# Batch 0 of an attention and feed-forward kernel in program order, with w_out converted by column halves

## The chip, the cores and the metric

The kernel runs on 1 core of one Trainium2 chip. The metric is the device time of one execution in microseconds. TensorE is called PE, VectorE DVE, ScalarE ACT, GpSimd POOL and SyncE SP, as in the profile.

## The reference

```
S = 448; scores = q @ k.T / sqrt(64) - log(S)          # 8 batches, 12 heads, head size 64
attn = 1 / (1 + exp(-scores))
x = (attn @ v)  as [8*448, 768]                        # heads side by side
h = x @ w_in                                           # w_in 768 x 2048
out = (h - tanh(h)) @ w_out                            # w_out 2048 x 768
```

q, k, v are 32-bit floats. w_in and w_out arrive as 64-bit floats; the kernel reads them as pairs of 32-bit words.

## The kernel before

**Stages.** For each batch there is the attention (six pairs of heads, the four 112-row chunks of the keys per pair), a first product h = x @ w_in with the function g = h - tanh(h) (`mix`, L691: six passes on ACT and six on DVE for a pair of 128-column blocks, 448 tokens each), and a second product g @ w_out (`moe2`, L723: three tiles of 128 tokens, then the last 64 tokens as `por`). From batch 1 on, each 32-bit operand is split into two 16-bit parts with a power-of-two scale, and a product takes three 16-bit matmuls (batch 1 still has its product with v in 32 bits, AV32). Batch 0 has its attention and its first product in 32-bit matmuls, because the weights aren't there yet: they are loaded and converted during batch 0.

**Conversion of the weights** (`convert`, L190). A piece is loaded by SP (`conv_load`), ACT takes the absolute value of its high words (`conv_sign`, L143), DVE puts the bits together in three passes (`conv_bits`, L148, L149, L152), and its squares are taken for the scales. w_in has 24 pieces of 128 x 512; their squares are made alternately on POOL and ACT and summed by columns on PE (`cn`, L181). w_out has 32 pieces of 128 x 384, whose squares are summed by rows on ACT (L161). Each call of `next` on this generator does one step: it loads piece t and carries earlier pieces one stage on. Once a scale is known, `split` (L202) makes the two 16-bit parts of a piece: the first on ACT or DVE, the rest on DVE.

**Order.** Batch 0's attention (`attention32`) and first product (`moe1` with split=False) are written as generators, woven with the conversions by estimated costs (`weave`), and the order of the instructions on each engine is left to a planner. Everything from `first` on stands under `manual_schedule`, where PE, ACT, DVE and POOL get their instructions in the order of the program; SP, which starts the loads and stores, is always planned. The attention of batch b + 1 is a generator of blocks (`stream`, L410): five steps prepare the first two pairs of heads (loads, norms, scales, the parts of K and Q), then each block does the scores of two key chunks of a pair, their Sigmoid, the product with v of the two before, and part of the preparation of the next pair. `first` does three blocks, the scale of w_out (`w_out_scales`, L249) and the first splits. `second` (L871) then runs `moe2` step by step: after step n all events with a position up to n are done. Events are blocks (BLOCKS0 for batch 0), splits of w_in (SPLIT: position of the first, distance) and the scales of the next batch's x (`batch_scales`, L583). The splits of w_out stand in `moe2` itself, one row block per step (`ahead`).

**Buffers that matter.** PSUM has two pairs of banks for scores and ph (tag sc), two banks for po, products of batch 0's attention and norms (mm), one for transposes (tr) and one for the products with v (av). SBUF tag t has eight large buffers for Sigmoids and the passes of `mix`.

In batch 0's first product (L652) the transpose of the column sums of w_in (`w_in_scales`, L228) comes after the first pair of blocks in the program, and its second half with the scale of g (`g_scales`) in the second pair.

## Time and profile before

| | us |
|---|---|
| median of 3 runs | 1292.35 (1292.14 to 1292.64) |
| profiled execution | 1291.75 |
| its span | 1289.9 |
| first ph of batch 0 starts | 78.98 |
| first po of batch 0 starts | 196.89 |
| first ph of batch 1 starts | 303.29 |

The span runs from the first to the last instruction. L12 is line 12 of the kernel; kT, qT, sc, acc, ph, po and por are PSUM tiles, named by what writes them. In rows of a timeline stand the start, the length, the engine, the line, the operation with output and inputs, the count, and in brackets the idle time before with what ended it. In rows of a group the two numbers after the bar are the busy time in total and the mean of one in ns, then the idle time before them.

### The profile page before, as it was taken

What the parts mean: (1) busy time and instruction counts of PE and PEld (TensorE: products, weight loads), DVE (VectorE), ACT (ScalarE), POOL (GpSimd) and SP (SyncE); (2) the same over time, 40 slices, a digit from 0 to 9 for tenths busy, and PEclk for the clock granted to TensorE, in tenths of its full rate; (3) what the DMA queues carried; (4) which work ended last, traced back from release to release, by engine and by line L of the source; (5) the groups of instructions that cost most, each with busy time, mean ns of one, the idle gap of its engine ahead of it and who ended that gap; (6) DMA issues with size and microseconds to landing.
All of it is one profiled execution on the core that took longest, in us unless ns stands there. A gap on an engine that the chain in (4) does not pass through costs nothing.

```text
span 1289.9 us, 20436 instructions
## 1 busy us (share of the span) xinstructions
PE 1246.1 (97%) x7997; PEld 686.3 (53%) x7997; DVE 949.6 (74%) x1479; ACT 944.6 (73%) x1358; POOL 50.9 (4%) x50
## 2 busy tenths in 40 slices
PE   9899849989999999999999999999999999999998
PEld 3234425545555655555555655556555655555555
DVE  4889978785976879667976769667985779735940
ACT  6768868866888768886888868886888868763830
POOL 1210000100000000100001000000000000000000
PEclk9899959999999999999999999999999999999999
DMA  9863421211012200221012200221002210100001
GB/s 255 249 184 118 149 58 44 64 42 40 1 49 64 56 7 6 66 64 41 1 33 72 62 9 1 62 65 48 1 23 67 52 34 1 28 13 19 1 13 32
DMA packets 113888, 70.53 MB, mean 55 GB/s; under 512 B 91776, under 2 KB 103552, under 8 KB 113792
## 3 DMA queue, kind: packets, MB, share of 16 engines
q1 hardware_dynamic: 113792, 69.23, 20.0%
q8 instruction: 63, 1.03, 0.3%
q14 instruction: 33, 0.27, 0.1%
HBM read 58.20 MB, written 11.01 MB: 54 GB/s over the span
## 4 chain that ended last, share of the span: by engine, by line
PE 84%; DVE 7%; ACT 4%; issue 3%; DMA 1%; SPq 1%; ACTq 0%; DVEq 0%
PE ph L661 30%; PE po L752 29%; PE sc L345 8%; PE acc L369 7%; PE por L770 5%; PE acc L379 1%; PE kT L282 1%; PE qT L282 1%; DVE stb L149 1%; ACT a L354 1%; DVE wo L209 1%; DVE sta L149 1%; DVE wo L152 1%; PE sc L554 1%; DMA rawo<-moe_w_out 1%
## 5 line engine op out<-in xcount | busy, mean ns | idle before, releaser
L752 PE MATMUL po<-wo,g 128*128 128x384 f16 x2304 | 389.8, 326 | 1.8 <-ACT o L761 1.0
L661 PE MATMUL ph<-xhl,wi 128*128 128x448 f16 x2016 | 382.6, 352 | 0.0
L752 PEld LDWEIGHTS <-g 128*128 128x128 f16 x2304 | 219.6, 98 | 172.5 <-issue 32.0
L661 PEld LDWEIGHTS <-wi 128*128 128x128 f16 x2016 | 196.7, 98 | 185.0 <-issue 2.1
L354 ACT ACTIVATE a<-sc,nls,rn 112x896 f32<-112x896 f32 x168 | 179.7, 1095 | 72.4 <-PE sc L345 72.4
L361 DVE SCALAR_TENSOR_TENSOR ahl<-a,ahl 112x896 f16<-112x896 f32 x144 | 155.9, 1123 | 61.2 <-ACT ahl L360 61.2
L697 ACT ACTIVATE u<-ph,ih 128x896 f32<-128x896 f32 x64 | 64.4, 1006 | 96.1 <-PE ph L661 96.1
L360 ACT ACTIVATE ahl<-a 112x896 f16<-112x896 f32 x144 | 128.1, 939 | 0.0
L345 PE MATMUL sc<-Q,K 64*112 64x448 f16 x1008 | 116.9, 365 | 0.0
L701 DVE SCALAR_TENSOR_TENSOR m<-ph,ihk,u 128x896 f32<-128x896 f32 x64 | 73.4, 1146 | 58.0 <-ACT th L699 57.7
L369 PE MATMUL acc<-ahl,vhl 112*64 112x448 f16 x864 | 96.5, 357 | 0.1
L635 ACT ACTIVATE g<-m,Sg 128x896 f16<-128x896 f32 x64 | 66.7, 1042 | 38.6 <-DVE m L715 31.5
L323 DVE SCALAR_TENSOR_TENSOR Q<-qT,sn,Q 128x448 f16<-128x448 f32 x42 | 28.6, 682 | 75.8 <-ACT Q L320 75.8
L652 PE MATMUL ph<-x,wi 128*128 128x448 f32 x192 | 75.3, 551 | 6.7 <-DVE th L702 6.7
L715 DVE COPY_PREDICATED m<-u,th 128x896 f32<-128x896 uint32 x64 | 77.3, 1208 | 5.8
L636 DVE SCALAR_TENSOR_TENSOR g<-m,Sg,g 128x896 f16<-128x896 f32 x64 | 73.3, 1145 | 7.8 <-ACT g L635 7.8
L345 PEld LDWEIGHTS <-K 64*112 64x112 f16 x1008 | 60.4, 129 | 34.0 <-issue 4.5
L712 DVE SCALAR_TENSOR_TENSOR m<-q,m 128x896 f32<-128x896 f32 x64 | 69.9, 1092 | 6.8 <-DVE m L708 0.5
L702 DVE SCALAR_TENSOR_TENSOR th<-ph,ih,th 128x896 f32<-128x896 f32 x64 | 73.1, 1143 | 0.0
L708 DVE SCALAR_TENSOR_TENSOR m<-q,m 128x896 f32<-128x896 f32 x64 | 69.4, 1084 | 0.0
L369 PEld LDWEIGHTS <-vhl 112*64 112x64 f16 x864 | 43.3, 109 | 47.9 <-issue 26.0
L714 ACT ACTIVATE u<-u,b 128x896 f32<-128x896 f32 x64 | 66.6, 1041 | 1.8
(129 smaller groups left out, 1359.4 us busy)
## 6 DMA issues: line engine op xcount, KB each, us to landing
raw<-moe_w_in SPq DMA_DIRECT2D x24, 512.0 KB, 5.6
rawo<-moe_w_out SPq DMA_DIRECT2D x32, 384.0 KB, 3.5
kn<-k SPq DMA_DIRECT2D x96, 112.0 KB, 2.9
qn<-q SPq DMA_DIRECT2D x96, 112.0 KB, 2.9
vn<-v SPq DMA_DIRECT2D x48, 224.0 KB, 2.7
out<-o SPq DMA_DIRECT2D x8, 336.0 KB, 3.2
out<-o SPq DMA_DIRECT2D x8, 288.0 KB, 3.1
out<-o SPq DMA_DIRECT2D x8, 240.0 KB, 2.6
```

Of the source, the lines that this page charges most:

```text
L345: nc.tensor.matmul(ps[:CK, h, :S], K[r, w, cs], Q[r, x, :], start=(n == 0), stop=(n == len(prods) - 1))
L354: nc.scalar.activation(a, ps[:CK, :, :S], AF.Sigmoid, bias=self.nls[:CK], scale=scale)
L360: nc.scalar.activation(A[:, 0], a, AF.Copy, scale=A_SCALE)
L361: nc.vector.scalar_tensor_tensor(A[:, 1], a, A_SCALE, A[:, 0], op0=ALU.mult, op1=ALU.subtract)
L369: nc.tensor.matmul(acc[h * D : (h + 1) * D, : self.S], v[:, w, h, c, :], A[:, x, h], start=(c == 0 and n == 0), stop=(c == 3 and n == 2),)
L636: nc.vector.scalar_tensor_tensor(g[:, 1], m, Sg, g[:, 0], op0=ALU.mult, op1=ALU.subtract)
L652: nc.tensor.matmul(ph[:, e, :S], self.where("in", c)[:, f * P : (f + 1) * P], xhl[c], start=(c == 0), stop=(c == self.NC - 1),)
L661: nc.tensor.matmul(ph[:, e, :S], self.wi[:, c * self.NB + k, part, e * P : (e + 1) * P], xhl[c][:, x, :], start=(i == 0), stop=(i == 3 * s ...
L701: V.scalar_tensor_tensor(m, ps, ihk, u, op0=ALU.mult, op1=ALU.mult)
L702: V.scalar_tensor_tensor(th, ps, ih, th, op0=ALU.mult, op1=ALU.subtract)
L715: V.copy_predicated(m, u.bitcast(U32), th)
L752: nc.tensor.matmul(po[e][:, :H], gs[f // 2][:, x, f % 2, tk * P : (tk + 1) * P], self.wo[:, 2 * f + e, w], start=(f == 0 and n == 0), stop ...
```

## The change

All of batch 0 comes under `manual_schedule`: its attention, its first product (now `moe1_32`, a function of its own) and the passage are written out in the order in which each engine gets them, with the steps of the conversion at fixed places, and `weave` is gone. An ACT instruction at the very start loads the table for Sigmoid. K of batch 0 is copied from PSUM by DVE and Q by ACT (both by ACT before), and the transposes of Q use a bank of tag mm. Of the squares of w_in, a quarter are made on POOL. w_out lies in SBUF by column halves (row e * 16 + f where it was 2 * f + e; `where` follows), and its pieces are converted in that order: the first half within attention and first product, the second half within the second product, into buffers of tag t. The squares of w_out are gone: PE sums the absolute values by columns instead (`wl`, the high 16 bits of the converted piece times ones), and `w_out_scale` makes a scale for each half. The second product of batch 0 runs by column halves, one bank and three tiles each; its outputs are stored by halves, by ACT alone. In batches 1 to 7 only the factors of the outputs change: one per half. All splits of w_in have their first part on ACT. The five preparing steps of `stream` stand at pairs 0 and 3 to 6 of the first product; `first` does four blocks, and twelve follow in BLOCKS0.

```diff
-    LATE = 0.86
-    NMY = 3000
-    PACE = 1.1
-    INIT = 5
-    SPLIT = 13, 0.6
+    INIT = (0, 3, 4, 5, 6)
+    SPLIT = 13, 0.8
+    CONV = 0.9
...
-    BLOCKS0 = (3, 7, 11, 16, 19, 22, 25, 28, 32, 36, 44, 48, 52)
-    WI = 1.25
+    BLOCKS0 = (2, 4, 7, 10, 13, 16, 19, 23, 27, 36, 43, 50)
...
         for c in range(self.NC):
             for i in range(4):
                 yield ("in", c, i, n)
-        for f in range(self.NF):
-            for i in range(2):
+        for i in range(2):
+            for f in range(self.NF):
                 yield ("out", f, i, self.HALF)
...
             p["raw"] = self.stage.tile([P, n], U64, name="raw", tag="raw", bufs=5)
         else:
             pool, tag, bufs = (self.op, "o", 2) if p["k"] % 5 % 3 == 1 else (self.att, "vhl", 3)
+            if i:
+                pool, tag, bufs = self.tp, "t", self.TP
             p["raw"] = pool.tile([P, n], U64, name="rawo", tag=tag, bufs=bufs)
...
         if not p["staged"]:
-            junk = self.sm.tile([P, p["piece"][3]], BF16, name="sqo", tag="sq", bufs=4)
-            nc.scalar.activation(junk, p["F"], AF.Square, accum_out=self.won[:, k : k + 1])
             return
-        pool, tag, bufs = (self.stage, "ssq", 2) if k % 3 == 2 else (self.sm, "sq", 4)
-        p["sq"] = pool.tile([P, p["piece"][3]], BF16, name="sq", tag=tag, bufs=bufs)
-        if k % 2:
+        p["sq"] = self.sm.tile([P, p["piece"][3]], BF16, name="sq", tag="sq", bufs=4)
+        if k % 4 == 1:
             nc.gpsimd.tensor_tensor(p["sq"], p["F"], p["F"], op=ALU.mult)
         else:
             nc.scalar.activation(p["sq"], p["F"], AF.Square)
     def conv_end(self, p):
+        kind, r, i, n = p["piece"]
         if not p["staged"]:
+            if r == 0:
+                self.wl = self.ps.tile([P, 512], F32, name="wl", tag="mm", bufs=2)
+            high = p["a"].bitcast(BF16).rearrange("p (n t) -> p n t", t=2)[:, :, 1]
+            self.nc.tensor.matmul(self.wl[:, :n], self.onesb, high, start=(r == 0), stop=(r == self.NF - 1))
             return
-        kind, r, i, n = p["piece"]
...
     def convert(self, part):
-        stages = [self.conv_load, None, self.conv_sign, self.conv_bits, self.conv_norm, None, None, self.conv_end]
         ps = []
         for k, (q, staged) in enumerate(part):
             ps.append({"piece": q, "k": k, "staged": staged})
+        end = [self.conv_norm, None, self.conv_end] if ps[0]["staged"] else [self.conv_end]
+        wait = [None] * (1 if ps[0]["piece"][2] else 2)
+        stages = [self.conv_load] + wait + [self.conv_sign, self.conv_bits] + end
...
     def split_w_in(self):
         for n in range(self.NC * self.NB):
-            self.split(self.wi, n, self.Swi, n % 4 > 0)
+            self.split(self.wi, n, self.Swi, True)
             yield 1
...
-    def w_out_scales(self):
+    def w_out_scale(self, e):
+        V = self.nc.vector
+        m = self.sm.tile([P, 1], F32, name="mo")
+        V.tensor_reduce(m, self.wl[:, : self.HALF], axis=AX.X, op=ALU.max)
         total = self.sm.tile([P, 1], F32, name="wtot2")
-        self.nc.vector.tensor_reduce(total, self.won, axis=AX.X, op=ALU.add)
-        pw = self.ps.tile([P, 512], F32, name="pw", tag="tr", bufs=1)
-        self.nc.tensor.matmul(pw[:, :1], self.onesf, total, start=True, stop=True)
-        self.Swo, self.iSwo = self.scale_of(pw[:, :1], "swo")
-    def split_w_out(self):
-        for f in range(self.NF):
-            for e in range(2):
-                self.split(self.wo, 2 * f + e, self.Swo, e == 0 or f % 2 == 1)
+        V.scalar_tensor_tensor(total, m, 1.05, m, op0=ALU.mult, op1=ALU.mult)
+        S, inv = self.scale_of(total, f"swo{e}")
+        self.Swo.append(S)
+        V.tensor_copy(self.iSwo[:, e : e + 1], inv)
+        h = slice(e * D, (e + 1) * D)
+        V.tensor_copy(self.iSwo[h, 2:3], inv[h])
+    def split_w_out(self, e):
+        for f in range(0, self.NF, 2):
+            for n in (f, f + 1):
+                self.split(self.wo, e * self.NF + n, self.Swo[e], n % 4 > 0)
             yield 1
...
-                t = self.transpose(loaded[j][n], name + "T")
+                t = self.transpose(loaded[j][n], name + "T", *((), ("mm", 2))[n])
                 o = self.qk.tile([P, S], F32, name=name + "S", tag=name)
-                nc.scalar.activation(o, t, AF.Copy)
+                if n:
+                    nc.scalar.activation(o, t, AF.Copy)
+                else:
+                    nc.vector.tensor_copy(o, t)
...
-        yield 0
+        self.warm(14)
         qk = {0: prep(0)}
-        self.warm(14)
-        yield 900
+        self.warm(4)
...
-                yield 1520
+                next(weights, None)
                 if len(todo) > 2:
                     av()
-                    yield 760
                 if c == 1 and j + 1 < NP:
                     qk[j + 1] = prep(j + 1)
                     if j + 2 < NP:
                         loaded[j + 2] = load(j + 2)
-                    yield 900
+                if c == 3 and 0 < j < NP - 1:
+                    next(weights, None)
+                if c == 3 and j == NP - 1:
+                    next(rest)
         while todo:
+            next(weights, None)
+            next(rest)
             av()
-            yield 760
...
+    def moe1_32(self, xs, rest):
...
+        for k in range(self.NF // 2):
+            ph = self.ps.tile([P, 2, 512], F32, name="ph", tag="sc", bufs=2)
+            for e in range(2):
+                f = 2 * k + e
+                for c in range(self.NC):
+                    nc.tensor.matmul(
+                        ph[:, e, :S],
+                        self.where("in", c)[:, f * P : (f + 1) * P],
+                        xs[c],
+                        start=(c == 0),
+                        stop=(c == self.NC - 1),
+                    )
+                if e == 0 and k == 1:
+                    next(w, None)
                     self.Sg, self.iSg = self.g_scales(m)
...
+                if e == 0 and k in self.INIT:
+                    next(self.blocks)
+                for _ in range(2 if e and 0 < k < 4 else 1):
+                    next(rest, None)
+            g = self.gp.tile([P, 2, 2, S], F16, name="g", tag="g")
+            self.gs.append(g)
+            self.tail = self.mix(ph[:, :, :S], g, self.ih0, self.ihk0)
+            if k == self.NF // 2 - 1:
+                return
+            for _ in self.tail:
+                pass
+            if k == 0:
+                w = self.w_in_scales()
+                next(w)
+                m = self.token_norms(self.ps.tile([P, 512], F32, name="nm0", tag="mm", bufs=2))
...
-        for _ in range(2):
-            next(ahead, None)
         nt = S // P
...
+        def products(po, tk, f, e):
+            for n, (x, w) in enumerate(prods):
+                for i in e:
+                    nc.tensor.matmul(
+                        po[i][:, :H],
+                        gs[f // 2][:, x, f % 2, tk * P : (tk + 1) * P],
+                        self.wo[:, i * self.NF + f, w],
+                        start=(f == 0 and n == 0),
+                        stop=((f, n) == last),
+                    )
+        if b == 0:
+            for e in range(2):
+                for tk in range(nt):
+                    po = {e: self.ps.tile([P, 512], F32, name="po", tag="mm", bufs=2)}
+                    for f in range(0, self.NF, 2):
+                        products(po, tk, f, (e,))
+                        products(po, tk, f + 1, (e,))
+                        if f + 2 == self.NF:
+                            if (e, tk) == (1, 0):
+                                nc.vector.tensor_scalar(iK[:, 1:], self.iSwo[:, 1:], self.iSg, None, op0=ALU.mult)
+                            o = self.op.tile([P, H], F32, name="oh", tag="o", bufs=2)
+                            nc.scalar.activation(o, po[e][:, :H], AF.Copy, scale=iK[:, e : e + 1])
+                            store(o, tk * P, P, slice(e * H, (e + 1) * H))
+                        yield 980
...
-        with tc.tile_pool(name="stage", bufs=2, reuse_waits="tile") as self.stage:
-            weights = self.convert([(q, True) for q in pieces[:nA]])
-            first = self.attention32(0, weights)
-            next(first)
-            self.warm(20)
-            self.weave((nA + 6, weights), (78000 * self.LATE, first))
...
-        self.gp = self.tc.alloc_tile_pool(name="gp", bufs=self.NF // 2, reuse_waits="tile")
-        nB = len(pieces) - nA
-        self.won = self.sm.tile([P, nB], F32, name="won", bufs=1)
-        first, rest = self.moe1(st, False), self.convert([(q, False) for q in pieces[nA:]])
-        self.blocks = self.stream()
-        init = (0.06 if k else 0.45 for k, _ in enumerate(itertools.chain((0,), itertools.islice(self.blocks, self.INIT))))
-        self.weave((54000.0, first), ((nB + 6) * self.PACE, rest), (1.0, init), until=first)
-        for _ in itertools.chain(rest, init):
-            pass
         E = mybir.EngineType
         with tc.manual_schedule(engines={E.PE, E.Activation, E.DVE, E.Pool}):
-            self.first()
+            nc.scalar.activation(const("one", 0.0), self.nls, AF.Sigmoid)
+            rest = self.convert([(q, False) for q in pieces[nA : nA + self.NF]])
+            with tc.tile_pool(name="stage", bufs=2, reuse_waits="tile") as self.stage:
+                self.attention32(0, self.convert([(q, True) for q in pieces[:nA]]), rest)
+            self.gp = tc.alloc_tile_pool(name="gp", bufs=self.NF // 2, reuse_waits="tile")
+            self.blocks = self.stream()
+            self.moe1_32(self.xs, rest)
+            for _ in rest:
+                pass
+            self.first(self.convert([(q, False) for q in pieces[nA + self.NF :]]))
             for b in range(1, self.B):
                 self.batch(b)
...
-    def first(self):
-        n = 3
-        next(self.blocks)
-        self.w_out_scales()
-        ahead = self.split_w_out()
-        for _ in range(n - 1):
-            next(ahead)
+    def first(self, rest):
+        n = 4
+        next(self.tail)
+        self.w_out_scale(0)
+        ahead = [self.split_w_out(0)]
+        for k in range(n):
             next(self.blocks)
+            for _ in range(2):
+                next(self.tail, None)
+            if k == 2:
+                self.finish_g()
+                next(ahead[0])
+        next(rest)
+        next(ahead[0])
+        next(rest)
...
         split = self.split_w_in()
         at, each = self.SPLIT
         events = [(at + k * each, lambda: next(split, None)) for k in range(self.NC * self.NB + 1)]
-        self.second(0, self.BLOCKS0, 2 * self.NP - n, events, ahead)
+        events += [(k + 0.5, lambda: next(ahead[0], None)) for k in range(self.NF // 2 - 1)]
+        steps = self.NF + 2
+        events += [(k * self.CONV, lambda: next(rest, None)) for k in range(1, steps + 1)]
+        at = math.ceil(steps * self.CONV)
+        def scale():
+            self.w_out_scale(1)
+            ahead[0] = self.split_w_out(1)
+        events += [(at, scale)] + [(at + 0.5 * k, lambda: next(ahead[0], None)) for k in range(1, self.NF // 2 + 1)]
+        self.second(0, self.BLOCKS0, 2 * self.NP - n, events)
```

More of the change, by code (lines that the diff above doesn't have):

```diff
@@ L1 @@
-import itertools
 import math
@@ L668, in moe1 @@
                         i += 1
-                if e == 0:
-                    if k == 1 and not split:
-                        next(w, None)
-                        self.Sg, self.iSg = self.g_scales(m)
-                    yield 3400
             g = self.gp.tile([P, 2, 2, S], F16, name="g", tag="g")
@@ new lines, in moe2 @@
+        if b == 0:
[12 more added lines that the diff above has]
+                        yield 980
+        else:
+            for tk in range(nt):
+                po = [self.ps.tile([P, 512], F32, name=f"po{e}", tag="mm", bufs=2) for e in range(2)]
+                for f in range(self.NF):
+                    products(po, tk, f, (0, 1))
+                    if f == self.NF - 1:
+                        o = self.op.tile([P, self.DM], F32, name="o", tag="o", bufs=2)
+                        nc.scalar.activation(o[:, :H], po[0][:, :H], AF.Copy, scale=iK[:, 0:1])
+                        nc.vector.tensor_scalar(o[:, H:], po[1][:, :H], iK[:, 1:2], None, op0=ALU.mult)
+                        store(o, tk * P, P, slice(0, self.DM))
+                    yield 980
@@ L869, in batch, with second @@
         self.second(b, blocks, self.ALONE, events)
-    def second(self, b, blocks, alone, events, ahead=iter(())):
+    def second(self, b, blocks, alone, events):
         step = lambda: next(self.blocks)
```

105 lines of the change are left out of this document (33 added, 72 removed).

## The prediction

> **What bounds the kernel now.** I cut the span where the work of batch 0 changes kind and read the busy times per stretch first: attention of batch 0, its first product, the passage to its second product, that second product, and the other seven batches.
>
> ```profile
> 0.00:79.00 79.00, 71.67 (x307) 22.94 (x307) 55.10 (x90) 54.30 (x80) 18.78 (x22) 0.91 0.84 237
> 79.00:162.20 83.20, 76.48 (x207) 37.96 (x203) 78.00 (x147) 67.10 (x133) 0.00 (x0) 0.98 0.49 146
> 162.20:196.90 34.70, 16.10 (x81) 8.91 (x82) 24.30 (x46) 24.30 (x43) 0.00 (x0) 0.61 0.24 58
> 196.90:303.30 106.40, 101.75 (x727) 56.65 (x726) 85.97 (x191) 82.49 (x154) 4.83 (x4) 0.98 0.21 53
> 303.30:1289.90 986.60, 980.11 (x6686) 559.86 (x6684) 706.26 (x1008) 716.36 (x950) 27.30 (x24) 1.00 0.13 32
> ```
>
> The columns are the length, then PE, its weight loads, DVE, ACT, POOL, the granted clock, the DMA share and GB/s. From 303.3 us on PE is busy 980.1 of 986.6 us at full clock, and the change leaves that part as it is; I price it at nothing and look at the first 303.3 us only. There the third stretch stands out: 34.7 us with PE busy for 16.1 at a clock of 0.61. The timeline of PE shows what it waits for.
>
> ```profile
> 139.01 9.26 PE L652 MATMUL ph<-x,wi 128*128 128x448 f32 x24 [1.62 <-DVE th L702]
> ...
> 151.31 10.84 PE L652 MATMUL ph<-x,wi 128*128 128x448 f32 x24 [2.75 <-DVE th L702]
> 168.45 0.59 PE L299 MATMUL pbn<-ss,onesf 112*128 112x2 f32 x2 [6.30 <-ACT sqn L291]
> ```
>
> Between the last ph (151.31 + 10.84) and 168.45 PE waits 6.3 us for the norms of batch 1. The preparation of batch 1 (norms, scales, K and Q) stands behind the unfinished mixes of batch 0 and the 32 conversions of w_out on DVE and ACT: DVE was busy 78.0 of 83.2 us in the first product, so its end is late, and PE pays for it afterwards. The change spreads just this. What it pays with is order: in the part it takes over, a PE instruction that waits for DVE holds all that stand behind it.
>
> **Stage 1, attention (79.0 us now).** The bound is the conversion of w_in on DVE, with the loads close behind.
>
> ```profile
> L148 DVE TENSOR_SCALAR sta<-sta 128x512 uint32<-128x512 uint32 x24 | 12.6, 527 | 20.9 <-ACT sta L143 20.9
> L387 DVE COPY x<-acc 128x448 f32<-128x448 f32 x6 | 3.7, 617 | 0.9 <-PE acc L379 0.9
> ```
>
> ```profile
> 9.99 0.43 DVE L148 TENSOR_SCALAR sta<-sta 128x512 uint32<-128x512 uint32 x1 [8.79 <-ACT sta L143]
> ...
> 29.63 0.42 DVE L148 TENSOR_SCALAR sta<-sta 128x512 uint32<-128x512 uint32 x1
> 30.09 0.71 DVE L149 SCALAR_TENSOR_TENSOR sta<-raw,sta 128x512 uint32<-128x512 uint32 x1
> 30.83 0.69 DVE L152 SCALAR_TENSOR_TENSOR wi<-raw,sta 128x512 uint32<-128x512 uint32 x1
> 31.44 0.42 DVE L148 TENSOR_SCALAR sta<-sta 128x512 uint32<-128x512 uint32 x1
> 31.89 1.41 DVE L149 SCALAR_TENSOR_TENSOR sta<-raw,sta 128x512 uint32<-128x512 uint32 x1
> ```
>
> ```profile
> 31.67 1.09 POOL L166 TENSOR_TENSOR sq<-wi 128x512 bf16<-128x512 f32 x1 [3.69 <-DVE wi L152]
> ```
>
> One piece takes 1.81 us from start to start (29.63 to 31.44), and 0.7 more when a POOL instruction runs beside it (1.41 against 0.71). The change squares 6 pieces on POOL instead of 12, so with the 4 sums of x2 some 10 such collisions stay: 24 x 1.81 + 10 x 0.7 = 50.4; the 6 copies of x (0.62) stay and 6 copies of K come over from ACT, which I price by the same row, since both read 448 columns from PSUM: 12 x 0.62 = 7.4. That is 57.8 us of DVE, a little over the 55.1 it was busy. The gain is in the 20.9 us that it idles for the Abs on ACT, 8.8 of them before the first piece. The new order puts the bits of a piece four score steps after its load, so I put the first ones at 14 us instead of 9.99 (my choice; the bounds take 10 to 18), and from there DVE needn't wait: it ends its last piece at 14 + 57.8 - 0.6 = 71, and the last scores and products follow: 73 us, a gain of 6. Bounds: none if the loads set the pace (a DMA share of 0.84 now, and 0.91 if the same bytes move in 73 us), 10 if the bits start as early as now. SP has its w_in loads one step apart with the same five buffers, and three w_out loads at the end; none is asked for later than now.
>
> **Stage 2, first product (83.2 us now).** PE needs 8 x 9.26 = 74.1 (row at 139.01). Two things are new in PE's queue. First, after the first pair of blocks stands the transpose of the column sums of w_in, which needs two reductions that DVE reaches only after the whole mix of that pair. Batch 1 runs the same mix in program order, and shows its length.
>
> ```profile
> 310.31 1.01 ACT L697 ACTIVATE u<-ph,ih 128x896 f32<-128x896 f32 x1 [7.04 <-PE ph L661]
> ```
>
> ```profile
> 317.88 0.19 DVE L613 TENSOR_SCALAR hb<-m,W 128x1 f32<-128x1 f32 x1
> ...
> 319.53 1.15 DVE L701 SCALAR_TENSOR_TENSOR m<-ph,ihk,u 128x896 f32<-128x896 f32 x1
> ...
> 326.21 1.14 DVE L701 SCALAR_TENSOR_TENSOR m<-ph,ihk,u 128x896 f32<-128x896 f32 x1
> ```
>
> ```profile
> 79.31 0.68 DVE L233 TENSOR_REDUCE st<-cn 128x1 f32<-128x512 f32 x1
> 79.91 0.68 DVE L234 TENSOR_REDUCE st<-cn 128x1 f32<-128x512 f32 x1
> 80.61 0.36 DVE L148 TENSOR_SCALAR stb<-stb 128x384 uint32<-128x384 uint32 x1
> 81.00 0.56 DVE L149 SCALAR_TENSOR_TENSOR stb<-rawo,stb 128x384 uint32<-128x384 uint32 x1
> 81.59 0.56 DVE L152 SCALAR_TENSOR_TENSOR wo<-rawo,stb 128x384 uint32<-128x384 uint32 x1
> ```
>
> From the end of the block (u starts at 310.31) to the end of the mix (317.88) are 7.6 us, the reductions (79.31 to 80.61) take 1.3: PE stands for 9 us, and the queue of ph behind it with it. The pass after it starts at a low clock, as the one at 151.31 did: 10.84 - 9.26 = 1.6. Second, the column sums of w_out: each piece's matmul waits for DVE's bits of the step before. Per pair DVE has the mix, 6.7 us (319.53 to 326.21), and two or three pieces of 1.5 us (80.61 to about 82.1), 9.7 to 11.2 us, plus 0.6 to 2.1 for K and Q of batch 1 in three of the pairs (passes by the 0.62 of L387, small steps by the 0.19 at 317.88): over the six pairs 2 to 7 it is 66.6 us if PE follows it fully, and 59.4 if PE runs free (6 x (9.26 + 0.64), the sums and transposes among it). So the stage is 9.3 + 9.5 + 11.3 + 59.4 to 66.6, or 89.5 to 96.7, against 83.2 with its 6.7 us of waits. DVE interleaved two pieces at 1.2 us each in the old order, which the new one can't, so I take the side nearer to DVE, 94: a loss of 11. Bounds: a loss of 6 to 14.
>
> One rule bears on the 1.6. The Trainium skill (TensorE: Matmul & The Clock Gate, Part 1) says that the clock halves only after an idle window of about 3.4 us and comes back after as long a busy one. The row at 151.31 slowed after 2.75 us, so here the measurement decides; by the page the next stage, whose gaps I put below 2.8 us, would lose nothing, and would be 1 us shorter than I take it.
>
> **Stage 3, passage to the second product (34.7 us now).** The preparation is done within stage 2 (four loads, norms, scales at pairs 0, 3 to 6), so what remains is the last mix and four blocks of batch 1, with ACT the longest queue.
>
> ```profile
> 167.08 1.32 ACT sqn L291 x4
> ```
>
> ```profile
> L354 ACT ACTIVATE a<-sc,nls,rn 112x896 f32<-112x896 f32 x27 | 28.9, 1095 | 12.5 <-PE sc L345 12.5
> ```
>
> Up to the first needed split, ACT has six Sigmoids of 1.07 (28.9 / 27), seven passes of the mixes at about 1 (the row at 310.31), two norms of 1.3, and two Q, a square and a split at half a microsecond (an estimate by their width, 448 and 384 columns against the 896 of 310.31): 18 us. With its waits for PE and the last g and split on DVE behind it (2 us) it is 20, and 1 more for the clock, which fell after 2.75 us at 151.31: 21, a gain of 14. Bounds: a gain of 10 to 17. It does four blocks where the old passage did three, so one block goes from stage 4.
>
> **Stage 4, second product (106.4 us now).**
>
> ```profile
> 240.91 3.10 PE L752 MATMUL po<-wo,g 128*128 128x384 f16 x18
> 243.84 0.28 PE L299 MATMUL pbn<-ss,onesf 112*128 112x3 f32 x2
> ...
> 247.42 3.10 PE L752 MATMUL po<-wo,g 128*128 128x384 f16 x18
> ...
> 287.59 0.95 PE L282 MATMUL qT<-ident,qn 112*128 112x112 f32 x4 [3.56 <-issue]
> ```
>
> ```profile
> rawo<-moe_w_out SPq DMA_DIRECT2D x32, 384.0 KB, 3.5
> ```
>
> 18 matmuls of po take 2.93 us (240.91 to 243.84), 0.163 each, so a step of six is 0.98; a block of batch 1 takes 3.6 (243.84 to 247.42). The column halves keep the number of matmuls and of weight loads: no cost. PE loses one block (-3.6) and gains 16 column sums of the same 384 columns (16 x 0.163 = +2.6), so its 101.75 busy us become about 100. DVE had 86.0 of 106.4. It gains 16 pieces of 1.5 (+23.5) and the scale of the second half (a reduction of 0.7 and seven small steps of 0.19: +2), and loses one block (two passes over K and four small steps: -2), 12 halves of w_in (-4.1, an estimate by the 0.36 at 80.61) and 3 outputs (-1.8, by the 0.62 of L387), both to ACT: 103.6 us, most of the new work in the first 17 of 48 steps. There it has some 45 us against PE's 40, and PE follows, by the column sums and by the splits, which are made only two steps ahead. Later it has slack, and the stall of 3.56 us at 287.59 (the transposition waits for K, that for the split of x on DVE) goes as the blocks come earlier. One bank less for po until the sums are read costs about 1 us at two changes of tile. I take 100 for PE, and 9 more for following DVE and the two changes: 109, a loss of 3. Bounds: a gain of 3 (PE free) to a loss of 9 (the loads land 3.5 us after issue and are asked for only two steps ahead, behind the loads of K and Q on SP, so ACT may stand for some).
>
> **Sum.** -6 + 11 - 14 + 3 = -6. The profiled execution took 1291.75 us, 1.85 above its span, and the median is 1292.35; with -6 that is 1285.75 and 1286.35. I say 1286.0. A measurement of this kernel tells about 0.2%, 2.6 us, from no change.
>
> **Rivals.** (a) PE runs free in stages 2 and 4, DVE's pieces falling beside it: -10 + 6 - 15 - 2 = -21, 1271. For it: DVE still had 20.4 us of idle in stage 4. Against: 103.6 of 109 us is little room for a queue in order. (b) Slower: DVE in the second product keeps the idle that it has now (106.4 - 86.0 = 20.4 us, mostly waits for ACT's half of a split or of Q). Then the stage is 103.6 + 20.4 = 124, a loss of 17.6, and the total -6 + 11 - 14 + 17.6 = +8.6, 1301. It decides from 116 us for that stage on, that is from 12 us of idle. For it: ACT gets 16 Abs and 12 halves of w_in more; against: much of that idle is where DVE is ahead. (c) The change does not what it says: the loads hold stage 1 at 79 and PE follows DVE fully in stage 2: 0 + 13.5 - 14 + 3 = +2.5, 1294; the work of batch 0 has only moved.
>
> **How the numbers follow.** The forecast has 0.45, (a) 0.2, (b) 0.2, (c) 0.15. The terms' bounds put the forecast's own case at 1277 to 1293; of it I count 0.36 faster, 0.06 no change, 0.03 slower. With (a) all faster, (b) 0.17 slower and 0.03 the same, (c) 0.02, 0.09, 0.04: faster 0.58, same 0.18, slower 0.24. The range takes in (a)'s centre and (b)'s: 1270 to 1300.
>
> **What would show it.** Right: the passage between the last ph of batch 0 and its first po near 21 us; one idle of PE of about 9 us, ended by DVE's reduction, after the first 24 ph; ph groups about 11 us apart after it; DVE above 9 tenths through the first third of the second product. Wrong: attention still at 79, no such idle, or a second product past 116 us.

## The result, and the profile after

The changed kernel takes 1306.74 us (median of 4 runs, 1304.88 to 1310.43) against 1292.24 for the kernel before beside it (4 runs, 1290.54 to 1292.64): a ratio of 1.0118, 95% interval 1.0094 to 1.0142. It is slower by 1.2%; forecast was 1286.0. The profiled execution took 1306.94 us with a span of 1305.1, 15.2 longer than before.

The same five stretches of the changed kernel, cut at the same events (first ph of batch 0, its last ph, first po, first ph of batch 1). The columns are again the length, then PE, its weight loads, DVE, ACT, POOL, the granted clock, the DMA share and GB/s:

```profile
0.00:78.38 78.38, 64.66 (x291) 20.36 (x291) 53.75 (x94) 53.13 (x79) 12.27 (x16) 0.93 0.88 246
78.38:173.35 94.97, 80.94 (x235) 41.09 (x234) 75.54 (x122) 50.74 (x69) 0.00 (x0) 0.96 0.24 69
173.35:194.18 20.83, 15.72 (x93) 7.37 (x91) 13.97 (x27) 19.52 (x29) 0.00 (x0) 0.84 0.23 55
194.18:318.30 124.12, 106.45 (x717) 57.25 (x715) 105.18 (x234) 93.65 (x183) 4.93 (x4) 0.93 0.32 93
318.30:1305.10 986.80, 980.14 (x6686) 559.79 (x6684) 706.66 (x1008) 716.96 (x950) 27.30 (x24) 1.00 0.13 32
```

| stage | before | forecast | after |
|---|---|---|---|
| attention | 79.0 | 73 | 78.4 |
| first product | 83.2 | 94 | 95.0 |
| passage | 34.7 | 21 | 20.8 |
| second product | 106.4 | 109 | 124.1 |
| the rest | 986.6 | 986.6 | 986.8 |

Two terms of the sum came out as worked out, two did not: attention gave 0.6 us instead of 6, and the second product cost 17.7 instead of 3. The timeline of PE in the changed kernel shows the first two stages.

```profile
76.42 0.38 PE L184 MATMUL cn<-sq,onesb 128*32 128x512 bf16 x1 [2.10 <-ACT sq L166]
...
78.38 9.29 PE L697 MATMUL ph<-x,wi 128*128 128x448 f32 x24
95.93 0.37 PE L241 MATMUL pt<-ident,st 128*1 128x128 f32 x1 [8.27 <-DVE st L238]
...
96.84 5.97 PE L697 MATMUL ph<-x,wi 128*128 128x448 f32 x12
```

The stand behind the transposition is there (8.27 us, forecast 9), and so is the slow half pair after it (5.97 us, where a half pair at full clock takes 4.67). In the second product PE waits at these places:

```profile
206.15 0.33 PE L176 MATMUL wl<-stb,onesb 128*128 128x384 bf16 x1 [2.51 <-DVE stb L150]
...
255.15 0.35 PE L310 MATMUL pbn<-ss,onesf 112*128 112x3 f32 x2 [1.57 <-DVE x L398]
...
262.03 3.25 PE L390 MATMUL acc<-a,vn 112*64 112x448 f32 x8 [4.19 <-ACT tn L312]
...
288.24 2.45 PE L380 MATMUL acc<-ahl,vhl 112*64 112x448 f16 x12 [3.83 <-ACT tn L312]
```

The waits for bits (2.51 is the longest of them, 5.8 in all) were forecast. The two waits for tn were not. pbn, the small matmul of the norms, and acc, the product of the attention weights with V, use the same bank of PSUM; tn on ACT is what reads pbn, so acc can't start until ACT has come to it. ACT's timeline ahead of each of the two:

```profile
255.98 1.61 ACT L211 ACTIVATE wo<-wo,swo_s 128x384 f16<-128x384 f32 x3
...
259.93 1.11 ACT L211 ACTIVATE wo<-wo,swo_s 128x384 f16<-128x384 f32 x2
260.94 0.90 ACT L211 ACTIVATE wi<-wi,swi_s 128x256 f16<-128x256 f32 x2
261.73 0.25 ACT L312 ACTIVATE tn<-pbn,tiny 128x3 f32<-128x3 f32 x1
...
283.44 0.58 ACT L800 ACTIVATE oh<-po,iK 128x384 f32<-128x384 f32 x1 [4.85 <-DVE iK L798]
283.92 2.09 ACT L211 ACTIVATE wi<-wi,swi_s 128x256 f16<-128x256 f32 x5
287.53 0.51 ACT L211 ACTIVATE wi<-wi,swi_s 128x256 f16<-128x256 f32 x1 [1.52 <-DVE wi L214]
287.94 0.24 ACT L312 ACTIVATE tn<-pbn,tiny 128x3 f32<-128x3 f32 x1
```

At 255.15 pbn is issued; tn comes 6.6 us later, behind eleven splits of w_out and w_in. The second time ACT first stands 4.85 us for the scale iK of the output copy, which DVE makes among the splits of x, and six halves of w_in then go ahead of tn.

### The profile page after: what moved, and what is told of

The parts are those of the page before. It is cut to its first block, busy times and chain, and to the rows that moved or that the text cites. A ratio compares the mean times of both kernels' runs of the same rounds, so it can differ in the third digit from the quotient of the medians.

```text
span 1305.1 us, 20440 instructions
## 1 busy us (share of the span) xinstructions
PE 1247.9 (96%) x8011; PEld 685.9 (53%) x8011; DVE 955.1 (73%) x1484; ACT 934.0 (72%) x1309; POOL 44.5 (3%) x44
## 4 chain that ended last, share of the span: by engine, by line
PE 84%; DVE 9%; ACT 3%; issue 2%; DMA 1%; SPq 0%; DVEq 0%; ACTq 0%
PE ph L667 29%; PE po L781 27%; PE sc L356 7%; PE acc L380 7%; PE por L819 5%; PE ph L697 3%; PE kT L293 1%; PE acc L390 1%; DVE sta L150 1%; PE qT L293 1%; DVE stb L150 1%; PE sc L567 1%; DVE wo L214 1%; ACT a L365 1%; DVE wi L214 1%
## 5 line engine op out<-in xcount | busy, mean ns | idle before, releaser
L781 PE MATMUL po<-wo,g 128*128 128x384 f16 x2304 | 393.8, 328 | 3.1 <-ACT o L810 1.0
L747 DVE COPY_PREDICATED m<-u,th 128x896 f32<-128x896 uint32 x64 | 77.3, 1208 | 6.6
```

The lines of the kernel that those rows point to most:

```text
L747: V.copy_predicated(m, u.bitcast(U32), th)
L781: nc.tensor.matmul(po[i][:, :H], gs[f // 2][:, x, f % 2, tk * P : (tk + 1) * P], self.wo[:, i * self.NF + f, w], start=(f == 0 and n == 0) ...
```

## The experiments

All times are medians beside runs of the kernel before on the same chip (1290.99 to 1292.24). The stages come from each kernel's profile. Attention alone varies from 76.4 to 79.2 us among the twelve kernels that leave it as it is, in part with the start of DVE's first bits (at 13.1 us in the shortest, 14.3 in the longest), so a difference in time below 3 us is read from the stages only. Each stage comes from a single profiled execution. "Rest" is from the last ph of batch 0 to the first of batch 1, passage and second product together.

| kernel | attention | first product | rest | time | ratio to before, 95% |
|---|---|---|---|---|---|
| changed | 78.4 | 95.0 | 145.0 | 1306.74 | 1.0094 to 1.0142 |
| scales early | 78.7 | 90.5 | 144.1 | 1301.26 | 1.0053 to 1.0086 |
| scales before mix | 76.4 | 87.4 | 145.7 | 1298.14 | 1.0039 to 1.0079 |
| sums later | 79.0 | 91.3 | 145.7 | 1303.03 | 1.0077 to 1.0109 |
| x copies on ACT | 72.3 | 95.6 | 143.7 | 1300.63 | 1.0061 to 1.0091 |
| 36 halves on ACT | 78.4 | 94.9 | 142.7 | 1304.79 | 1.0089 to 1.0125 |
| iK early | 77.3 | 94.9 | 142.5 | 1303.83 | 1.0083 to 1.0115 |
| splits later | 76.9 | 95.2 | 142.2 | 1303.10 | 1.0079 to 1.0109 |
| w_out spread | 78.1 | 95.2 | 141.5 | 1303.06 | 1.0079 to 1.0109 |
| pbn in another bank | 77.5 | 94.9 | 140.5 | 1300.30 | 1.0055 to 1.0085 |
| tn between blocks | 76.5 | 95.0 | 139.2 | 1301.46 | 1.0065 to 1.0098 |
| half the bits cut | 77.0 | 94.9 | 138.1 | 1300.58 | 1.0053 to 1.0084 |

### The first product: is the stand a matter of place?

```diff
-            if k == 0:            # after the mix of the first pair
-                w = self.w_in_scales(); next(w); m = self.token_norms(...)
+                if e == 0 and k == 0:   # after the first half of the first pair
+                    w = self.w_in_scales(); next(w); m = self.token_norms(...)
```

> The reductions of the column sums of w_in, the transposition behind them and the norms of x are issued after the first half of the first pair instead of after that pair's mix; nothing else is changed. Theory (the stand is only a matter of place): in the changed kernel PE stands 8.27 us for the reduction and runs the next half pair at a low clock (5.97 us instead of 4.67). DVE is idle for 7.8 us ahead of that mix, so the reductions fit there. The first product falls from 94.8 to about 86 us and the time from 1306.7 to about 1298. Rival (DVE sets the pace of the whole product): PE stands as long, spread over the sums of w_out that wait for DVE; the product stays at 92 or more and the time at 1304 or more.

```diff
-                if e == 0 and k == 1:
+                if e == 1 and k == 0:   # besides: the second part ahead of the mix
                     next(w, None); self.Sg, self.iSg = self.g_scales(m)
```

> As with the early scales, and the second part of them too (the maximum behind the transposition, the two small matmuls and the scale of g) is issued ahead of the first pair's mix, after the second half of that pair. Theory (a matter of place): with only the first part early PE still stood 3.34 us for that maximum, which DVE reached after the mix, and ran the next half pair at a low clock; with both parts early nothing of PE is behind that mix, the first product falls from 94.9 (90.5 with the first part) to 86 or 87, and the time from 1306.7 to about 1298. Rival (DVE sets the pace): DVE has the same work in front of PE's next sums, the product stays at 90 or more, 1301.

With the first part alone half of the stand moves to the next instruction that DVE reaches only after the mix:

```profile
97.19 0.38 PE L246 MATMUL pb<-mx,onesf 1*128 1x1 f32 x2 [3.34 <-DVE mx L244]
```

With both, no wait for a reduction is left, and two for the bits come in their place, this one and one of 1.12 us right after it:

```profile
97.35 0.33 PE L176 MATMUL wl<-stb,onesb 128*128 128x384 bf16 x1 [1.30 <-DVE stb L150]
```

The stage falls by 7.6 of the 9.6 us that stand and clock cost: the theory holds, and the waits for bits, 7.9 us in the stage instead of 5.6, take back the remainder. The time falls by 8.6, but 2.0 of these lie in attention, which the edit leaves as it is.

```diff
-        end = ... else [self.conv_end]
+        end = ... else [None, self.conv_end]   # the column sum one step later
...
-        steps = self.NF + 2
+        steps = self.NF + 3
```

> The column-sum matmul of each piece of w_out is issued one step later, so that PE doesn't ask for DVE's bits of the step just before; nothing else. Theory (PE waits because its order puts the sum too close behind the bits): the waits of wl go, 5.5 us in the first product and 5.8 in the second, and the time falls by 7 to 10, to about 1298. Rival (DVE is the pace in both): PE runs ahead by a step and then waits for the mix to free a bank of ph, or for a split, by about as much; the time falls by 2 or less.

With the second line the scale of the second half of w_out and its splits also come a step later. The first product gains 3.7 of the 5.5 us that the theory had there, but the rest gains nothing. The waits of wl in the second product fall from 5.8 to 0.4 us, and PE meets DVE and ACT in the passage instead (2.79 us for a split Q) and at tn:

```profile
258.83 3.26 PE L390 MATMUL acc<-a,vn 112*64 112x448 f32 x8 [6.88 <-ACT tn L312]
```

Neither theory fits alone: in the first product it was PE's order, behind it the wait moved to something else.

### Attention: loads, or DVE's queue?

```diff
-            nc.vector.tensor_copy(x, acc[:, : self.S])
+            nc.scalar.activation(x, acc[:, : self.S], AF.Copy)
```

> In the attention of batch 0 the six copies of x out of PSUM are made by ACT instead of DVE; nothing else. Theory (DVE's queue is the pace of attention): DVE is busy almost without a gap from 24.7 to 73.7 us there; six copies of 0.62 go (3.7 us), and the three waits of PE for x (7.7 us), which stood behind a piece's bits, go too. Attention falls from 78.4 to 73 to 75 us, the time to about 1302. Rival (the loads set the pace, DMA share 0.88): DVE waits for the next piece instead, and attention stays above 77 us, the time within 2 us of 1306.7.

The stage falls to 72.3 us at a DMA share of 0.94, so the loads do not hold it at 78. The groups of DVE in attention, first of the changed kernel, then of this one (line, operation, tiles, count, then busy time, mean ns, idle time before them):

```profile
L149 DVE TENSOR_SCALAR sta<-sta 128x512 uint32<-128x512 uint32 x24 | 10.1, 422 | 6.8 <-ACT sta L144 6.7
L547 DVE COPY KS<-KT 128x448 f32<-128x448 f32 x6 | 3.7, 618 | 11.2 <-PE KT L293 11.2
L398 DVE COPY x<-acc 128x448 f32<-128x448 f32 x5 | 3.1, 618 | 0.0
```

```profile
L149 DVE TENSOR_SCALAR sta<-sta 128x512 uint32<-128x512 uint32 x24 | 12.4, 517 | 2.9 <-ACT sta L144 2.7
```

The copies are gone, and so are 4 us of waits for ACT's Abs. That DVE's queue holds the stage fits: attention takes 72.2 to 72.6 us in all four kernels with the copies on ACT. How it does so is less clear. PE's waits for x, which the theory expected to go, are still 5.1 us, now for ACT's copies, and the waits for Abs vary by themselves: they are 4.2 to 6.8 us in the twelve kernels without this edit and 2.9 to 4.3 in the four with it. The edit also moves the six copies of batch 1, in the passage and the second product.

### The second product: load, order, or a bank?

Four edits each take one suspect away.

```diff
-            self.split(self.wi, n, self.Swi, True)
+            self.split(self.wi, n, self.Swi, n % 4 > 0)
```

> Only one edit of the change is undone: of the 48 halves of w_in ACT makes 36, as before, and DVE the other 12. Theory A (ACT's queue is too long): PE's two waits for tn on ACT in the second product (4.19 and 3.83 us in the changed kernel) shrink to 3 us or less in all, and the time falls by about 6, to 1300. Theory B (DVE's backlog holds ACT too, since the halves alternate between them and DVE was busy for 62.6 of the first 67.8 us of this product): DVE gets 12 passes of about 0.4 us more, the two waits stay at 8 us or grow, and the time is 1306 to 1311.

```diff
-    SPLIT = 13, 0.8
+    SPLIT = 21, 0.64
```

> The splits of w_in start at step 21 of the second product instead of 13, with 0.64 steps between them instead of 0.8, so that they end at the same place; nothing else. Theory (DVE and ACT carry too much in the first 68 us of this product, where DVE is busy 62.6, and too little after it, 42.5 of 56): 10 to 13 splits, 0.43 us of each engine apiece, move behind the first wait for tn. That wait (4.19 us) falls below 1.5, and the time falls by 4 to 6, to about 1302. Rival (the shared bank and the place of tn alone): the first wait goes, the later ones grow by as much, and the time stays within 2 us of 1306.7.

```diff
         # moe2 of batch 0
-        if (e, tk) == (1, 0): <iK of the second half>   # at its first output
+        if (e, tk) == (1, 0): <iK of the second half>   # at its first matmul
```

> The scale of the second column half (iK) is computed on DVE eight steps earlier, ahead of the splits of x instead of among them. In the changed kernel ACT stands 4.85 us for it with the copy of an output (oh), with the halves of w_in and tn queued behind that copy, and PE stands 3.83 us for tn. Theory: this is what makes the second wait for tn; that wait goes with its slow clock, the first (4.19 us) stays, and the time falls by 4 to 6, to about 1302. Rival (the backlog of halves on both engines makes it): ACT's stand moves to the next half that waits for DVE, PE's wait stays above 2 us, and the time stays within 2 us of 1306.7.

```diff
-        pb = self.ps.tile([P, 512], F32, name="pbn", tag="av", bufs=1)
+        tag, bufs = ("mm", 2) if self.one_po else ("av", 1)
+        pb = self.ps.tile([P, 512], F32, name="pbn", tag=tag, bufs=bufs)
```

> Once the column sums of w_out have been read, the matmul of the norms (pbn) takes the free one of the two banks of po instead of the bank of acc; order and work stay. Theory (the bank): acc waits for tn only because tn must first read the bank that acc takes next. Then both waits of acc (4.19 and 3.83 us) and the slow clock behind them (about 4 us) go, and the time falls by 8 to 11, to about 1297. Rival (backlog): the queues of ACT and DVE are late by that much whatever bank is used, PE meets them again at the next scores, whose K or Q isn't split yet, and at least half of the gain is lost: 1302 to 1306.

The waits for tn that are left, one block of PE's timeline for each of the four kernels in that order:

```profile
261.40 3.26 PE L390 MATMUL acc<-a,vn 112*64 112x448 f32 x8 [4.68 <-ACT tn L312]
...
285.76 1.33 PE L380 MATMUL acc<-ahl,vhl 112*64 112x448 f16 x12 [1.79 <-ACT tn L312]
...
308.85 1.33 PE L380 MATMUL acc<-ahl,vhl 112*64 112x448 f16 x12 [2.34 <-ACT tn L312]
```

```profile
257.72 2.07 PE L390 MATMUL acc<-a,vn 112*64 112x448 f32 x8 [3.97 <-ACT tn L312]
284.51 2.45 PE L380 MATMUL acc<-ahl,vhl 112*64 112x448 f16 x12 [5.02 <-ACT tn L312]
```

```profile
260.87 3.25 PE L390 MATMUL acc<-a,vn 112*64 112x448 f32 x8 [4.19 <-ACT tn L312]
...
285.76 2.24 PE L380 MATMUL acc<-ahl,vhl 112*64 112x448 f16 x12 [2.52 <-ACT tn L312]
```

```profile
261.13 4.76 PE L782 MATMUL po<-wo,g 128*128 128x384 f16 x18 [2.90 <-ACT tn L313]
```

The 36 halves turn the second wait into two smaller ones (rest -2.3), but the waits for tn add up to 8.8 us instead of 8.0, as theory B had it. Moving the splits leaves the first wait and lengthens the second (rest -2.8); the early iK takes 1.3 off the second (rest -2.5, half of what its theory had). Much of these gains is the clock: PE's busy time in the stage is 103.4, 104.7 and 105.3 us instead of 106.4, for the same products. With pbn in the other bank the waits of acc are gone, but po now waits for that bank, and twice the next pbn (1.71 and 1.77 us) for po's output copy: rest -4.5, between the two expectations. No single suspect carries the loss. The next two ask about load against burst.

```diff
         # conv_bits, pieces of the second column half only
-        nc.vector.tensor_scalar(au, au, 3, ...)
-        nc.vector.scalar_tensor_tensor(au, p["lo"], 29, au, ...)
```

> For the second column half of w_out two of the three DVE passes of each piece's conversion are left out (the shift and the merge of the low word; 0.35 and 0.56 us, 16 pieces, 14.6 us of DVE in the second product), so that half of w_out has wrong bits; ACT, the loads and PE have the same work as in the changed kernel. Theory (DVE's work is the bound of the first 68 us of this product): the waits for its bits go (5.8 us), the queues of DVE and ACT are early at the first wait for tn (4.19 us with its clock), and the time falls by 9 to 13, to about 1296. Rival (the shared bank, ACT's queue or the order of the waits is the bound): the waits for tn stay, only those for the bits go, and the time falls by 5 or less.

```diff
-        events += ... (at + 0.5 * k, lambda: next(ahead[0], None)) ...
+        events += ... (at + 1.0 * k, lambda: next(ahead[0], None)) ...
```

> The splits of the second half of w_out come at a pair per step (steps 18 to 25 of the second product) instead of a pair per half step (17.5 to 21); nothing else. The runs so far left the first wait for tn at 4 to 5 us with 13 splits of w_in moved away and with 14.6 us of DVE's work cut, so the theory is now: tn stands behind this burst of 16 splits on ACT, which itself goes hand in hand with DVE. Then the first wait falls from 4.19 us to below 1.5, the second (3.83) stays, and the time falls by 4 to 6, to about 1302. Rival (the burst doesn't matter, the first wait comes of where tn is issued): the wait stays above 3 us, and the time within 2 us of 1306.7.

The stage of the kernel with the cut, and its waits:

```profile
192.78:310.02 117.24, 105.37 (x717) 57.33 (x715) 89.67 (x202) 93.11 (x183) 4.93 (x4) 0.93 0.33 98
```

```profile
253.63 3.26 PE L391 MATMUL acc<-a,vn 112*64 112x448 f32 x8 [4.35 <-ACT tn L313]
279.92 2.45 PE L381 MATMUL acc<-ahl,vhl 112*64 112x448 f16 x12 [3.84 <-ACT tn L313]
```

With 15.5 us less of DVE (89.67 busy against 105.18) the stage is only 6.9 shorter, between the two expectations: 5.8 of it are the waits for the bits, and those for tn stay. So DVE's load there is not what makes PE wait for tn. The spread splits fare little better: the first wait falls from 4.19 to 3.69 only, against the theory of the burst, while the clock and the 1.57 us before pbn improve (rest -3.5).

```diff
-        # i == 1: scales(g + 2) at the head of the block, pbn ahead of acc in the same bank
+        # after block i == 0:  self.mid = lambda g=g: scales(g + 2)
+        events += [(p + 1.5, lambda: self.mid()) for p in self.BLOCKS0]
```

> In the second product of batch 0 the matmul of the norms (pbn), tn and the scales behind it are issued 1.5 steps after the block before, when the bank of acc has just been read, instead of at the head of the block that needs the bank again; nothing else. Theory (place and bank): tn then has two to eight steps before acc takes the bank; both waits (4.19 and 3.83 us) and the low clock behind them (about 4 us) go, and so does the wait of pbn for the copy of x (1.57): the time falls by 8 to 11, to about 1297. Rival (the queues of ACT and DVE are late in themselves): PE waits as long for the scores or the split K a little later, and the time falls by 4 or less.

```profile
192.35:310.70 118.35, 102.46 (x716) 56.02 (x715) 104.60 (x234) 92.82 (x183) 4.95 (x4) 0.99 0.33 98
```

```profile
253.35 0.35 PE L310 MATMUL pbn<-ss,onesf 112*128 112x3 f32 x2 [3.51 <-DVE x L398]
...
296.45 0.39 PE L310 MATMUL pbn<-ss,onesf 112*128 112x3 f32 x2 [2.58 <-ACT x L400]
```

At the same load both waits for tn are gone and the clock is 0.99 instead of 0.93: the rest gains 5.8 us, the most of any edit of order in this product. The gain stays short of 8 to 11, since other waits come in their place: 3.51 us for the copy of x, which is behind the burst on DVE, 2.58 for another copy, and 1.54 before a transposition. All waits of PE in the stage fall from 17.5 to 15.9 us only; the other 4.0 us of the gain are PE's busy time, 102.46 instead of 106.45, at the better clock. The time gained 5.3, between theory and rival; by time pbn in another bank did no worse (1300.30 against 1301.46).

### Joined

The edits are those shown above: for the four, both of the scales, the early iK, the spread splits and tn between the blocks. The one new edit is the slower conversions':

```diff
-    CONV = 0.9
+    CONV = 1.1
```

> Four edits together: both parts of the scales of w_in ahead of the first mix, iK eight steps earlier, the splits of the second half of w_out at a pair per step, and the norms' matmul with tn between the blocks. Theory (the waits are separate, each one of place): -8.6 for the scales as measured, and the two waits for tn with their clock, -8 to -11, however many of the other three edits it takes: about 1288, 4 us below the kernel before. Rival (the backlog of DVE and ACT in the second product): only the first part adds up, the second gives 4 or less: 1294 or more.

> The four edits joined before, and the copies of x on ACT. Theory (each gain lies in a stage of its own): attention falls by 6 as it did alone, the rest stays as in the joined kernel, and the time is 1286 to 1287, below the kernel before by 0.35%. Rival (what attention gains is lost to a later load or to the fuller queue of ACT, whose x copies come in the second product too): 1290 or more, no difference from the kernel before.

> The same five edits, and the column sums of w_out a step later. Alone, this edit won 3.6 us in the first product and lost them in the passage and at the first wait for tn. Theory (PE's waits for the bits hold the second product): with the waits for tn out of the way the 5.3 us for the bits there go, the product falls from 118.5 to 114 or 115 and the time by 3 to 5 against the five edits alone, to about 1282. Rival (DVE's load): PE waits elsewhere for as long, the product stays at 116 or more, and the time within 2 us of the five edits alone.

> The same five edits, and the conversions of the second half of w_out 1.1 steps apart instead of 0.9, so that they end at step 20 instead of 17 and the splits start there. Theory (DVE's load in the first third of the second product is what PE waits for): DVE has 16 pieces of 1.5 us over 20 us of steps instead of 16, the waits for the bits fall from 5.3 to 2 or less, and the time by 3 against the five edits alone. Rival (it is the distance of the sum from its bits, one step whatever the pace): the waits stay at 4 or more, and the time within 2 us.

| kernel | attention | first product | passage | second product | time | ratio to before, 95% |
|---|---|---|---|---|---|---|
| four edits | 79.2 | 87.8 | 20.8 | 118.5 | 1292.49 | 0.9997 to 1.0017 |
| and x copies on ACT | 72.2 | 87.3 | 21.0 | 115.4 | 1286.89 | 0.9954 to 0.9978 |
| and sums later | 72.6 | 82.7 | 25.8 | 111.0 | 1280.94 | 0.9910 to 0.9944 |
| five edits, conversions slower | 72.6 | 87.6 | 21.0 | 121.0 | 1292.78 | 0.9999 to 1.0020 |

The four edits came out at 1292.5, between theory (1288) and rival (1294), no difference from the kernel before: the first product gives 7.2 us and the rest 5.6 (139.4), no more than tn between the blocks gave alone, so that the early iK and the spread add nothing to it. With the copies of x on ACT the time is the 1286.9 that was expected. That it lies near the 1286.0 of my prediction is chance: this is another kernel, with a first product of 87.3 us where I had 94 and a second of 115.4 where I had 109. Nor did the rest stay as it was, which was expected: by the profiles attention gives 7.0 us and the second product 3.1, together more than the 5.6 by which the medians differ, because the profile of the four edits is of the slowest of its runs and that of the five of the fastest. With the sums a step later it is 1280.9, 0.7% below the kernel before: now that the waits for tn behind it are gone, the edit that was worth 3.7 us alone gives 6.0 (4.2 between the two profiles). It moves 4.8 us into the passage, where PE now comes before DVE and ACT, and takes 4.6 and 4.4 out of the two products; its second product went below the 114 that the theory had, and the waits for bits there from 3.4 us to 0.4. The second product of that kernel:

```profile
181.07:292.03 110.96, 103.38 (x716) 56.65 (x715) 97.95 (x222) 92.95 (x182) 4.57 (x4) 0.97 0.33 96
```

For the slower conversions neither expectation held: PE's waits for the bits rose from 3.4 to 5.8 us, as the rival had it, but the time rose by 5.9, which neither expected. The second product is 5.6 us longer: PE's waits there add up to 15.2 us instead of 12.2, with 1.9 for DVE's splits of w_out instead of 0.5, and its busy time is 2.9 us longer at a lower clock (0.96 against 0.99 in the stage). Why a slower pace makes the waits for the bits longer stays open.

## Why the prediction was wrong

**Stage 1 failed at "from there DVE needn't wait".** DVE started its first bits at 13.68 us, as put (14), and the work up to its last piece took some 4 us less than forecast. But it waited 6.7 us for ACT's Abs (the L149 group above), ended its last piece at 73.7 instead of 71, and from there to the first ph went 4.6 us instead of 2, with 2.10 for the last square on ACT (the row at 76.42). I had treated ACT as always ahead. As I read the rows it was caught in a ring: DVE's copy of x stood behind bits, PE's next products behind that copy (7.7 us in all), ACT's passes behind PE, DVE's bits behind ACT. That ring is not shown. What the runs show is that with the copies out of DVE's queue (3.1 us before the first ph) the stage comes to 72.2 to 72.6 us, near the 73 that I had put; how the remainder divides among the waits stays open.

**Stage 2 was right.** 95.0 against 94, with its two mechanisms at 8.27 and 1.3 us against 9 and 1.6. Its third term, PE following DVE, came to 5.6 us of waits for bits where 94 leaves 4.5. But part of that was the place of the sums and not DVE's pace, as the 3.7 us of the later sums show.

**Stage 3 was right.** 20.8 against 21, with ACT as the longest queue (19.5 of the 20.8 us busy). The clock fell there as I had taken it: PE waits 3.11 us for a Sigmoid, and the granted clock is 0.84 in the stage.

**Stage 4 failed at "100 for PE, and 9 more for following DVE and the two changes".** Of those 9, 7.9 were there: 5.8 us for the bits and 2.1 for splits and an output. PE's own work was 102.9 (busy time of the joined kernel with the copies on ACT, at a clock of 0.99) instead of 100; my own terms, 101.75 - 3.6 + 2.6, already gave 100.75. What I had not counted is PE standing for tn on ACT, 8.0 us, 1.6 for the copy of x ahead of pbn, and 3.6 of slow clock (106.45 against 102.9 busy). 102.9 + 7.9 + 8.0 + 1.6 + 3.6 is 124.0. In the kernel before, acc waited 0.3 us for tn in all of this stage (waits, in total, times, longest):

```profile
PE acc L379 <- ACT tn L301: 0.3, 1, 0.3
```

My sum had no term for it, though the change put the splits of the second half, iK and more halves of w_in in front of tn. Taking tn out of that place gave 5.8 us and not the 8.0 with their clock, so the waits behind it are part of the same loss; with the copies on ACT and the later sums as well the stage came to 111.0.

**Rival (b)** had the stage at 124 and the sum at +8.6, and the stage came out at 124.1 with 18.9 us of DVE idle (124.12 - 105.18) against the 20.4 it assumed. Its number was right, its mechanism was not, so the agreement is luck: with 15.5 us less work on DVE the idle time grew to 27.6 (117.24 - 89.67) instead of staying, and with the order mended the stage was 111.0 at 98 us of DVE. The sum missed (b)'s 1301 by what attention did not give. **Rival (c)** was right on attention's 78.4, but not because of the loads. **Rival (a)**, PE free, did not hold in this order of work.

## What to carry to other kernels

When a change puts more work into an order written by hand, list for every small instruction that frees a PSUM bank what now stands ahead of it in its own queue. A pass of a quarter of a microsecond (tn) held PE for 4 us twice, once behind eleven splits, once behind a copy that waited 4.85 us for its scale and the six splits after it. A load account per engine doesn't find this: cutting 15.5 us of DVE's work gave 6.9, issuing tn between the blocks gave 5.8 at the same load, 4.0 of it by the clock. And the gains of edits of order don't simply add up: the later sums gave 3.7 us while the waits for tn stood behind them, and 6.0 once these were gone.

## What the runs showed of the hardware

A wait of one and the same length at the same place may or may not cost the clock. In the changed kernel and in the one with the early scales PE waits 2.51 us for the same matmul, and runs the same work after it:

```profile
206.15 0.33 PE L176 MATMUL wl<-stb,onesb 128*128 128x384 bf16 x1 [2.51 <-DVE stb L150]
...
206.97 1.34 PE L356 MATMUL sc<-Q,K 64*112 64x448 f16 x12
208.24 1.72 PE L390 MATMUL acc<-a,vn 112*64 112x448 f32 x8
```

```profile
202.00 0.33 PE L176 MATMUL wl<-stb,onesb 128*128 128x384 bf16 x1 [2.51 <-DVE stb L150]
...
202.82 1.98 PE L356 MATMUL sc<-Q,K 64*112 64x448 f16 x12
204.74 2.72 PE L390 MATMUL acc<-a,vn 112*64 112x448 f32 x8
```

The second loses 1.6 us, and its clock falls only at 203.38, 1.4 us after the wait's end. The traces show where the difference comes from. In each of the seventeen, all changes of the granted clock lie on a grid of 3.41 us, whose place differs from trace to trace. These are the two steps of the grid around the wait in the changed kernel, then the step that holds most of it and the next one with the early scales (length, PE's busy time, clock, DMA share, GB/s):

```profile
201.84:205.25 3.41, 1.80 (x12) 1.00 0.71 224
205.25:208.67 3.42, 2.52 (x22) 1.00 0.25 83
```

```profile
199.97:203.38 3.41, 1.38 (x13) 1.00 0.55 206
203.38:206.80 3.42, 3.42 (x16) 0.50 0.49 90
```

In the changed kernel the wait is spread over two steps, with PE busy for 1.80 and 2.52 us, and the clock stays. With the early scales 2.03 us of it lie in one step, PE is busy for 1.38 of 3.41 us, and the next step runs at half clock. All steps of batch 0 in the seventeen traces, from 5 us on, say the same: all 82 at full clock in which PE was busy for less than 1.45 us were followed by half clock, of the 1181 with more than 2.0 us one was, and of the 91 between them 25. The Trainium skill (TensorE: Matmul & The Clock Gate, Part 1) says that the clock is set by a window of about 3.4 us that runs freely, so that the place of a change varies by its phase. The grid agrees with that; that PE's clock falls after a window in which it was busy for 1.38 us does not agree with the idle window that the prediction cites from there. For a forecast this means that a wait of some 2.5 us has a price between nothing and 1.6 us on this kernel, by where it falls on the grid, and that differences of 2 or 3 us between two profiles can be the clock alone.
